# GpSimd's integer sums of the weight conversion in four pieces of 256 columns each

## The chip, the core and the metric

The kernel runs as one program on one core of a Trainium2 chip. The metric is the device time of an execution in microseconds (us). A core has five engines that work through their own instruction queues in order: TensorE (PE in the profile, with PEld for its weight loads), VectorE (DVE), ScalarE (ACT), GpSimd (POOL) and SyncE (SP), which issues most of the DMA transfers here.

## What is computed

Three parts follow each other: attention in which each row keeps its 32 largest scores, a dense layer with a gate, and a layer with eight experts of which each token uses two.

```python
scores = scale * np.matmul(q, k.transpose(0, 1, 3, 2))          # 4 batches, 8 heads, 576 tokens, 64
kth = np.partition(scores, -32, axis=-1)[..., -32:-31]
scores = np.where(scores >= kth, scores, -1e9)
attn = np.exp(scores - max); attn = attn / (sum + 1e-09)
x = attn @ v                                                     # 2304 x 512
h = x @ w_in                                                     # w_in 512 x 2048
x = (h * np.clip(h + 3.0, 0.0, 6.0) / 6.0) @ w_out               # w_out 2048 x 512
logits = x @ w_gate + log1p(exp(x @ w_noise)) * noise            # top 2 of 8 experts per token
out[token] += weight * (np.maximum(x[token] @ w1[e], 0) @ w2[e]) # for its two experts e
```

`w_in` and `w_out` reach the kernel as 64-bit floats. [...]

## The kernel before

The program has a phase A (attention and the dense layer, about the first 880 us) and a phase B (the experts). A scheduler puts the instructions of each engine into a fixed order before the program runs. It places them by its own times for each instruction, so that a change of a few instructions may move many others.

Phase A goes in steps of one slot, 144 in all: a slot is one head for 128 tokens. In a step PE makes the scores (L295), ACT copies them (L304, tile `ss`), and DVE finds the 32 largest: seven maxima over segments (L313, `seg`), a chain of maxima and replacements (L319 to L323, tile `a`), a mask of what lies below (L340, `z`), a maximum over that (L352), the choice of the threshold (L356) and the masking of the exponentials (L365, `e`). GpSimd helps each step with small work: the bias of the exponential (L328, `a`), the product of mask and scores (L346, `y`), sums and reciprocals (L370, L373, `sum` and `rb`), and the low halves of values that are split into two fp32r numbers (L213 for `k`, L268 for `q`, L426 and L438 for the output of attention).

The dense layer goes in blocks of 128 of its 2048 hidden columns, 16 blocks (`fb`). Between steps 4 and 19 the weights of one block per step are converted by `Weights.convert`: two DMAs bring a tile `wraw` of 128 x 1024 pairs of words; DVE makes the upper word's bits (L117 with its result in `wt`, L118, twice each, 512 columns at a time); ACT turns the lower word into an integer (L120); GpSimd adds the two as integers (L121). Then `Weights.split` makes a rounded copy on ACT (L130) and what is left with two matmuls and a copy (L138 to L140). Eleven of the blocks are stored to DRAM (`wscr`) and loaded again by SP for each use (`w_fetch`, L450, tile `ws`, four buffers); five stay in SBUF. From step 25 on, PE works on one block of one group of tokens per step (L464 into `h`, L505 into `xa`) beside the attention. The loads of `k` (L203, L204), `v` (L218, L220) and `q` (L261) go through the same SP queue; a batch's eight heads of `k` are loaded at the steps where its first tokens come up.

Phase B multiplies the gathered tokens of each expert with its weights (L880, L904).

Of the kernel before, what the change touches and what calls it, by code (L numbers as in the profile page):

```python
# [13 lines left out]
ALU = mybir.AluOpType  # L14
# [61 lines left out]
class Weights:  # L76
# [27 lines left out]
    def convert(self, fb):  # L104


        if not self.f64:
            return
        nc, t = self.nc, self.raws[fb]
        if self.small:  # L110
            m = self.ap.tile([128, 1024], F32, name=f"wm{fb}", tag="wm", bufs=1)
            nc.vector.tensor_scalar(m.bitcast(I32), t[:, :, 1], 0x7FFFFFFF, None, op0=ALU.bitwise_and)
            nc.vector.tensor_scalar(m, m, TINY, None, op0=ALU.is_ge)
        for i in range(2):
            hi = t[:, 512 * i:512 * i + 512, 1]
            tmp = self.ap.tile([128, 512], I32, name=f"wt{fb}_{i}", tag="lx", bufs=LXB)
            nc.vector.tensor_scalar(tmp, hi, 3, 0x3FFFFFF8, op0=ALU.logical_shift_left, op1=ALU.bitwise_and)  # L117
            nc.vector.scalar_tensor_tensor(hi, hi, -0x40000000, tmp, op0=ALU.bitwise_and, op1=ALU.bitwise_or)  # L118
        lo = t[:, :, 0]
        nc.scalar.activation(lo, lo.bitcast(U32), AF.Copy, scale=2.0 ** -29)  # L120
        nc.gpsimd.tensor_tensor(t[:, :, 1], t[:, :, 1], t[:, :, 0], op=ALU.add)  # L121
        if self.small:

            nc.vector.tensor_tensor(t.bitcast(F32)[:, :, 1], t.bitcast(F32)[:, :, 1], m, op=ALU.mult)
# [1144 lines left out]
```

## Time and profile before

| what | value |
|---|---|
| median of 3 runs | 1406.64 us (1406.3 to 1410.03) |
| the profiled execution's own time | 1411.69 us |
| its span in the profile | 1409.9 us |
| PE busy | 1302.8 us (92% of the span) |
| DVE busy | 1004.1 us (71%) |
| POOL busy | 818.2 us (58%), 1151 instructions |
| ACT busy | 745.0 us (53%) |
| chain that ended last, by engine | PE 56%, DVE 26%, DMA 5%, POOL 4%, ACT 4% |

The span is what the profile covers, from the first instruction to the last; the execution's own time is 1.8 us longer. Shares over the whole span hide the stages: PE is the busiest engine over all, yet in the first 200 us it is not. So the rows below are mostly of stretches. A busy time counts an instruction from its start to its end, also while it is held up in the engine.

### The profile page before, as it was taken

To read this page: it belongs to the slowest core of one execution; us is meant where nothing else is said; L and a number is where in the kernel's file an instruction comes from. 1 tells how busy PE (TensorE), PEld (TensorE's weight loads), DVE (VectorE), ACT (ScalarE), POOL (GpSimd) and SP (SyncE) were. 2 spreads that over 40 slices of the span, in tenths; PEclk is the share of its full clock that TensorE was granted. 3 is DMA by queue.
4 is the path that set the end of the run, shared out by engine and by line. 5 is a ranking of instruction groups with operands and counts; after the bars stand their busy time and mean duration, and the time that the engine had idled before them with its cause. 6 is when DMAs were issued, how large, how long until landed. Compare 5 with 4: busy or idle time off the path is not lost.

```text
span 1409.9 us, 26993 instructions
## 1 busy us (share of the span) xinstructions
PE 1302.8 (92%) x9006; PEld 1128.9 (80%) x9006; DVE 1004.1 (71%) x3827; ACT 745.0 (53%) x1565; POOL 818.2 (58%) x1151
## 2 busy tenths in 40 slices
PE   5767899999999979999899999899999999999996
PEld 3545688888888868898688888778889888898985
DVE  7999997899998899986999983456353534444241
ACT  6867766667676756666676654435222322223220
POOL 7666666676666778665587864233214556465461
PEclk9888999999999989999999999999999999999998
DMA  7766645445355614445233547756446555465431
GB/s 234 262 242 218 250 170 196 155 144 172 130 179 193 222 12 156 163 171 200 70 128 136 150 143 257 236 167 210 134 147 193 170 171 188 146 216 174 144 110 38
DMA packets 138101, 239.57 MB, mean 170 GB/s; under 512 B 39779, under 2 KB 93155, under 8 KB 123872
## 3 DMA queue, kind: packets, MB, share of 16 engines
q1 hardware_dynamic: 127600, 210.57, 45.3%
q0 software_dynamic: 10352, 27.18, 5.8%
q8 instruction: 73, 1.20, 0.4%
q14 instruction: 76, 0.62, 0.1%
HBM read 209.08 MB, written 31.64 MB: 171 GB/s over the span
## 4 chain that ended last, share of the span: by engine, by line
PE 56%; DVE 26%; DMA 5%; issue 4%; POOL 4%; ACT 4%; SPq 1%; POOLq 0%; DVEq 0%; ACTq 0%
PE ac L904 15%; PE hb L880 15%; PE h L464 7%; PE xa L505 7%; DVE seg L313 5%; DVE e L365 5%; DVE a L352 4%; DVE z L340 3%; PE s L295 3%; PE av L416 3%; PE pa L384 2%; DVE a L356 2%; DVE r L480 1%; POOL idw L758 1%; PE et L844 1%
## 5 line engine op out<-in xcount | busy, mean ns | idle before, releaser
L904 PE MATMUL ac<-w,hh 128*128 128x512 f32 x960 | 249.0, 401 | 4.9 <-issue 3.6
L880 PE MATMUL hb<-xe,w 128*128 128x320 f32 (+2 forms) x1536 | 239.8, 311 | 1.0 <-DVE hh L887 0.5
L880 PEld LDWEIGHTS hb<-xe,w 128*128 128x128 f32 x1536 | 232.5, 189 | 10.1 <-issue 3.9
L346 POOL TENSOR_TENSOR y<-z,ss 128x576 f32<-128x576 bf16 x144 | 192.5, 1337 | 56.5 <-DVE z L340 49.6
L904 PEld LDWEIGHTS ac<-w,hh 128*128 128x128 f32 x960 | 173.5, 189 | 44.3 <-ACT hh L886 5.0
L887 DVE SCALAR_TENSOR_TENSOR hh<-hb,hh 128x640 fp32r<-128x640 f32 (+2 forms) x72 | 53.9, 749 | 213.6 <-ACT hh L886 176.7
L886 ACT ACTIVATE hh<-hb 128x640 fp32r<-128x640 f32 (+2 forms) x72 | 46.6, 647 | 292.2 <-PE hb L880 264.6
L313 DVE MAX8 seg<-ss 128x8 f32<-128x82 f32 (+1 forms) x1008 | 166.7, 228 | 20.6 <-ACT ss L304 20.2
L464 PE MATMUL h<-xT,ws 128*128 128x256 f32 x1188 | 164.2, 286 | 7.5 <-DVE r L480 7.4
L505 PE MATMUL xa<-ws,g 128*128 128x512 f32 x594 | 166.6, 404 | 1.9 <-ACT g L187 1.8
L464 PEld LDWEIGHTS h<-xT,ws 128*128 128x128 f32 x1188 | 149.3, 189 | 15.3 <-DVE r L480 12.3
L866 POOL TENSOR_TENSOR w<-r,w 128x1024 fp32r<-128x1024 f32 x40 | 98.4, 2465 | 84.5 <-ACT w L864 77.1
L365 DVE SCALAR_TENSOR_TENSOR e<-ss,thrs,e 128x576 f32<-128x576 f32 x144 | 141.3, 982 | 0.5
L335 ACT ACTIVATE e<-ss,a 128x576 f32<-128x576 f32 x144 | 113.9, 791 | 32.1 <-POOL a L328 30.9
L304 ACT COPY ss<-s 128x576 f32<-128x576 f32 x144 | 92.5, 642 | 65.3 <-PE s L389 45.8
L352 DVE MAX8 a<-y 128x8 f32<-128x576 f32 x144 | 108.0, 750 | 23.1 <-POOL y L346 22.9
L493 POOL TENSOR_TENSOR g<-r,g 128x256 fp32r<-128x256 f32 x124 | 96.1, 775 | 36.5 <-ACT g L187 23.1
L340 DVE TENSOR_SCALAR_CACHE_REDUCE z<-ss,a 128x576 bf16<-128x576 f32 x144 | 115.4, 801 | 1.0
L505 PEld LDWEIGHTS xa<-ws,g 128*128 128x128 f32 x594 | 102.2, 189 | 17.2 <-ACT g L187 2.1
L384 PE MATMUL pa<-ident,e 128*128 128x128 f32 x576 | 92.9, 285 | 24.1 <-DVE e L365 21.0
L295 PE MATMUL s<-kt,qt 128*128 128x288 f32 x512 | 102.0, 323 | 10.6 <-ACT ph L397 5.7
L920 POOL DMA_INDIRECT out_dram<-y,id x40 | 41.9, 1048 | 115.6 <-DVE y L919 91.6
(217 smaller groups left out, 2645.5 us busy)
## 6 DMA issues: line engine op xcount, KB each, us to landing
ws<-wscr SPq DMA_DIRECT2D x99, 1024.0 KB
r<-in_moe_w_dram SPq DMA_DIRECT2D x144, 256.0 KB
wscr<-wsp SPq DMA_DIRECT2D x11, 1024.0 KB
wraw<-in_moe_w_in_dram SPq DMA_DIRECT2D x16, 512.0 KB
wraw<-in_moe_w_out_dram SPq DMA_DIRECT2D x16, 512.0 KB
ck<-in_moe_w_in_dram SPq DMA_DIRECT2D x32, 256.0 KB
ck<-in_moe_w_out_dram SPq DMA_DIRECT2D x32, 256.0 KB
out_dram<-zero SPq DMA_DIRECT2D x18, 256.0 KB
```

Of the source, the lines that this page charges most:

```text
L295: nc.tensor.matmul(p[:, half, 0:288], qt[:, j, :], KT[b, h][:, half * 288:(half + 1) * 288], start=(m == 0), stop=(m == n - 1))
L313: nc.vector.max(ST[i][:, j, :], SS[i][:, edge[j]:edge[j + 1]])
L335: nc.scalar.activation(e, SS[i], AF.Exp, bias=A8[i][:, 24:25], scale=0.125)
L340: TS(z, SS[i], A8[i][:, 7:8], None, op0=ALU.is_lt, op1=ALU.add, accum_out=A8[i][:, 26:27])
L346: nc.gpsimd.tensor_tensor(y, Z.pop(i), SS[i], op=ALU.mult)
L352: nc.vector.max(A8[i][:, 8:16], Y.pop(i))
L365: STT(E[i], SS.pop(i), thrs[:, i:i + 1], E[i], op0=ALU.is_ge, op1=ALU.mult, accum_out=SUM[i // 2][:, i % 2:i % 2 + 1])
L384: nc.tensor.transpose(p[:, j * 128:(j + 1) * 128], e[:, j * 128:(j + 1) * 128], ident)
L464: o = nc.tensor.matmul(p[:, 0:n], w[:, a, d, :], xt[b][:, d, 0:n], start=(m == 0), stop=(m == 11))
L505: nc.tensor.matmul(ACC[t], g[:, a, j * 128:(j + 1) * 128], w[:, b, :], start=(fb == 0 and m == 0), stop=(fb == NFB - 1 and m == 2))
L880: o = nc.tensor.matmul(p[:, half, 0:hn], w[:, a, d, :], XE[job][:, b, d, half * hn:(half + 1) * hn], start=(m == 0), stop=(m == 11))
L904: o = nc.tensor.matmul(ACC[job, j], h[:, a, j * 128:(j + 1) * 128], w[:, b, :], start=(x % NF2 == 0 and m == 0), stop=(x % NF2 == NF2 - 1 ...
```

## The change

The one integer addition of 1024 columns per block becomes four of 256 columns.

```diff
         lo = t[:, :, 0]
         nc.scalar.activation(lo, lo.bitcast(U32), AF.Copy, scale=2.0 ** -29)
-        nc.gpsimd.tensor_tensor(t[:, :, 1], t[:, :, 1], t[:, :, 0], op=ALU.add)
+
+        for i in range(0, 1024, 256):
+            nc.gpsimd.tensor_tensor(t[:, i:i + 256, 1], t[:, i:i + 256, 1], t[:, i:i + 256, 0], op=ALU.add)
```

The columns, the values and the waits ahead of the first addition are the same. In the changed kernel each line from the addition on has a number higher by two: L123 is the addition, L348 is what was L346, and so on. A number behind a tile's name counts what was built and has no other meaning.

The order of GpSimd's queue around the blocks 4 and 5. Before:

```order
L328 TENSOR_SCALAR a83_397<-a83_397 128x1
L121 TENSOR_TENSOR wraw4_529<-wraw4_529 128x1024
L373 TENSOR_SCALAR rb0_416<-sum0_341 128x128
L346 TENSOR_TENSOR y2_364<-z2_339,ss2_251 128x576
L346 TENSOR_TENSOR y3_451<-z3_411,ss3_308 128x576
L213 TENSOR_TENSOR ksb0_103<-kr6_236,ksb0_103 128x4x64
L213 TENSOR_TENSOR ksb0_103<-kr6_236,ksb0_103 64x64
L328 TENSOR_SCALAR a84_486<-a84_486 128x1
```

With the change:

```order
L330 TENSOR_SCALAR a83_400<-a83_400 128x1
L372 TENSOR_SCALAR sum0_341<-sum0_341 128x2
L123 TENSOR_TENSOR wraw4_538<-wraw4_538 128x256 x2
L348 TENSOR_TENSOR y2_367<-z2_339,ss2_251 128x576
L123 TENSOR_TENSOR wraw4_538<-wraw4_538 128x256 x2
L375 TENSOR_SCALAR rb0_419<-sum0_341 128x128
L348 TENSOR_TENSOR y3_457<-z3_414,ss3_308 128x576
L330 TENSOR_SCALAR a84_492<-a84_492 128x1
```

The four pieces stand as two and two, with a product `y` between them (with an L375 or an L330 in other blocks); 12 of the 16 blocks have such a break, the others stand as four in a row.

The scheduler also moves work far behind the conversion, up to the last steps of phase A; phase B has the order that it had. PE's queue around the scores of the last slot (s143). Before:

```order
L464 MATMUL h7_8_12782<-xT7_10859,ws7_8_12523 128x256 x10
L295 MATMUL s143_12720<-kt31_9830,qt143_12643 128x288 x4
L389 MATMUL s143_12720<-ident_66,e138_12442 128x128
L464 MATMUL h7_8_12782<-xT7_10859,ws7_8_12523 128x256 x2
L505 MATMUL xa14_12256<-ws7_7_12435,g7_7_12775 128x512 x3
L505 MATMUL xa15_12260<-ws7_7_12435,g7_7_12775 128x512 x3
L674 MATMUL lg13_12894<-wgn_948,lx13_12844 128x16 x2
L384 MATMUL pa139_12725<-ident_66,e138_12442 128x128 x4
L674 MATMUL lg13_12894<-wgn_948,lx13_12844 128x16 x2
L464 MATMUL h7_9_12855<-xT7_10859,w9_1199 128x256 x12
```

With the change:

```order
L507 MATMUL xa14_12304<-ws7_8_12571,g7_8_12897 128x512 x3
L297 MATMUL s143_12768<-kt31_9878,qt143_12691 128x288 x4
L507 MATMUL xa15_12308<-ws7_8_12571,g7_8_12897 128x512 x3
L466 MATMUL h7_10_12953<-xT7_10907,ws7_10_12742 128x256 x11
L386 MATMUL pa139_12773<-ident_66,e138_12490 128x128 x4
L391 MATMUL s143_12768<-ident_66,e138_12490 128x128
L466 MATMUL h7_10_12953<-xT7_10907,ws7_10_12742 128x256
L507 MATMUL xa14_12304<-w9_1229,g7_9_12950 128x512
L665 MATMUL lt13_12887<-ident_66,xm13_12215 128x128 x4
```

`h7_10` is the dense layer's block 10 of token group 7. Before, the last scores stand within block 8, and block 9 follows; with the change block 10 follows.

SP's queue where a `k` of the last batch is loaded (kr25). Before:

```order
L203 DMA kr24_8761<-in_k_dram 128x256
L204 DMA kr24_8761<-in_k_dram 64x64
L450 DMA ws3_15_7384<-wscr_78 128x2048
L450 DMA ws4_1_7559<-wscr_78 128x2048
L203 DMA kr25_8852<-in_k_dram 128x256
L204 DMA kr25_8852<-in_k_dram 64x64
L261 DMA qr11_1_7645<-in_q_dram 128x4x64
```

With the change:

```order
L452 DMA ws3_14_7336<-wscr_78 128x2048
L205 DMA kr24_8809<-in_k_dram 128x256
L206 DMA kr24_8809<-in_k_dram 64x64
L205 DMA kr25_8900<-in_k_dram 128x256
L206 DMA kr25_8900<-in_k_dram 64x64
L452 DMA ws3_15_7432<-wscr_78 128x2048
L263 DMA qr11_1_7693<-in_q_dram 128x4x64
L452 DMA ws4_1_7607<-wscr_78 128x2048
```

The load of kr25 stood behind two loads of the dense layer's weights (ws3_15, ws4_1); it stands ahead of both now.

## Rows read from the trace of the kernel before

**Rows 1.** Busy time of each engine by stretch: us, PE, PEld, DVE, ACT, POOL, clock, DMA share, GB/s

```profile
50.00:157.00 107.00, 76.38 (x435) 52.53 (x434) 104.27 (x380) 78.26 (x151) 68.42 (x86) 0.87 0.64 228
335.00:840.00 505.00, 477.25 (x3887) 421.75 (x3885) 457.98 (x2087) 337.11 (x799) 351.46 (x589) 0.98 0.44 146
840.00:945.00 105.00, 98.35 (x603) 84.86 (x600) 42.60 (x126) 45.92 (x86) 35.27 (x62) 0.97 0.68 214
```

**Rows 2.** Single lines of DVE, whole span: ns shortest/median/longest, first and last start

```profile
L117 DVE TENSOR_SCALAR wt<-wraw x32: 396/422/2214, 9.1 to 148.6; 128x512 int32<-128x512 int32 x32
L118 DVE SCALAR_TENSOR_TENSOR wraw<-wraw,wt x32: 666/678/2072, 9.5 to 152.1; 128x512 int32<-128x512 int32 x32
L356 DVE SCALAR_TENSOR_TENSOR a<-rank,a x144: 201/230/2650, 24.5 to 837.1; 128x9 f32<-128x9 f32 x144
L365 DVE SCALAR_TENSOR_TENSOR e<-ss,thrs,e x144: 790/815/2743, 25.1 to 837.3; 128x576 f32<-128x576 f32 x144
L313 DVE MAX8 seg<-ss x1008: 215/228/249, 12.3 to 827.4; 128x8 f32<-128x82 f32 x120, 128x8 f32<-128x83 f32 x48
```

**Rows 3.** Timeline of DVE, from 53 to 148 us: start us, us, instruction

```profile
53.65 2.65 DVE L356 SCALAR_TENSOR_TENSOR a<-rank,a 128x9 f32<-128x9 f32 x1
...
62.40 1.65 DVE L118 SCALAR_TENSOR_TENSOR wraw<-wraw,wt 128x512 int32<-128x512 int32 x1
...
100.35 1.85 DVE L356 SCALAR_TENSOR_TENSOR a<-rank,a 128x9 f32<-128x9 f32 x1
...
107.30 1.05 DVE L356 SCALAR_TENSOR_TENSOR a<-rank,a 128x9 f32<-128x9 f32 x1
...
124.96 1.67 DVE L117 TENSOR_SCALAR wt<-wraw 128x512 int32<-128x512 int32 x1
...
132.04 1.23 DVE L365 SCALAR_TENSOR_TENSOR e<-ss,thrs,e 128x576 f32<-128x576 f32 x1
...
145.24 2.34 DVE L365 SCALAR_TENSOR_TENSOR e<-ss,thrs,e 128x576 f32<-128x576 f32 x1
```

**Rows 4.** Timeline of POOL at three of these places

```profile
53.97 0.45 POOL L426 TENSOR_TENSOR xs<-xs 128x128 f32<-128x128 f32 x1
54.39 1.88 POOL L121 TENSOR_TENSOR wraw<-wraw 128x1024 int32<-128x1024 int32 x1
...
61.42 2.08 POOL L121 TENSOR_TENSOR wraw<-wraw 128x1024 int32<-128x1024 int32 x1 [2.60 <-ACT ksb L187]
63.46 1.73 POOL L346 TENSOR_TENSOR y<-z,ss 128x576 f32<-128x576 bf16 x1
...
146.93 0.97 POOL L426 TENSOR_TENSOR xs<-xs 128x128 f32<-128x128 f32 x1
```

**Rows 5.** Single lines of POOL, whole span, columns as in rows 2

```profile
L121 POOL TENSOR_TENSOR wraw<-wraw x16: 1884/1894/2403, 11.8 to 153.5; 128x1024 int32<-128x1024 int32 x16
...
L268 POOL TENSOR_TENSOR qsb<-qr,qsb x36: 721/739/1384, 4.4 to 772.1; 128x256 fp32r<-128x256 f32 x36
...
L426 POOL TENSOR_TENSOR xs<-xs x72: 452/463/983, 54.0 to 849.9; 128x128 f32<-128x128 f32 x72
```

**Rows 6.** Chain of waits that ended last: start us, us, what

```profile
20.61 2.20 POOL wraw L121
...
837.20 1.68 PE h L464 x12
...
852.66 1.41 PE h L464 x12
854.07 1.39 PE xa L505 x6
```

**Rows 7.** Waits by total, 160 to 850 us: us, times, longest

```profile
DVE a L352 <- POOL y L346: 22.9, 22, 3.4
```

**Rows 8.** Timeline of SP's queue: ws3_15 and ws4_1, then kr25

```profile
464.41 3.98 SPq L450 DMA_DIRECT2D ws<-wscr  x2
470.52 0.33 SPq L203 DMA_DIRECT2D kr<-in_k_dram  x1
```

## The prediction

> **What bounds the kernel now.** I read the busy times by stretch first, to see which engine is full where the additions run. All 16 start between 11.8 and 153.5 us [rows 5]. From 50 to 157 us DVE is busy for 104.27 of 107 us, POOL for 68.42 and PE for 76.38 [rows 1]. In that stretch DVE sets the pace; GpSimd has a third of its time free. From 335 to 840 us PE (477 of 505) and DVE (458) are both nearly full and take turns, and from 840 to 945 us PE is full (98 of 105) [rows 1]. The chain of waits says the same: near 837 us it passes from DVE to PE and stays there for the rest of the dense layer [rows 6].
>
> Next I looked at what DVE's full time consists of, in the durations of single lines. L313 has 215 ns at its shortest and 249 at its longest. L356, which writes nine columns, takes 201 ns at its shortest and 2650 at its longest; L117 goes from 396 to 2214, L118 from 666 to 2072, L365 from 790 to 2743 [rows 2]. So some lines of DVE are held up inside the instruction and others never. The timelines show by what: L356 starts at 53.65 us and lasts to 56.30, and on POOL the addition runs from 54.39 to 56.27 [rows 3, 4]. DVE comes free when GpSimd's instruction ends. The other way round as well: the addition from 61.42 to 63.50 holds L118, L118 then runs, and the product behind the addition takes 1.73 us; behind the addition at 145 us L426 takes 0.97 where its shortest is 0.452 [rows 4, 5]. The two engines take turns at something that both use, an instruction at a time.
>
> From 50 to 157 us, seven of DVE's instructions are held by an addition. Each one's time less the shortest of its line [rows 2, 3]: 62.40: 1.65 - 0.67 = 0.98; 100.35: 1.85 - 0.20 = 1.65; 107.30: 0.85; 124.96: 1.67 - 0.40 = 1.27; 132.04: 1.23 - 0.79 = 0.44; 145.24: 2.34 - 0.79 = 1.55. At 53.65 other GpSimd work holds L356 too, so I count the addition's own 1.88 [rows 4]. The sum is **8.6 us** of the pacing engine's time.
>
> **The change, part by part.**
>
> Price of a piece. The trace has no integer addition of 256 columns. Below it cannot cost less than a quarter of the whole, 1.884 / 4 = 0.47 us. Above I take the other two-input operation of 256 columns, L268 with 0.72 [rows 5]. L426 with 128 columns takes 0.452 [rows 5], so 128 columns more cost 0.269 and a fixed share of 0.452 - 0.269 = 0.18 us is left. The addition's 1.884 less 0.18 makes 1.70 for 1024 columns, 0.43 for 256: a piece is **0.61 us**. It is the nearer value, being the addition's own rate per column. Four pieces take 2.44, 0.55 more than one addition; 16 x 0.55 = 8.8 us of POOL time (between 0 and 16 x 1.0 = 16). It lies in a stretch where GpSimd is idle for 38.6 of 107 us [rows 1], and the copy L130 on ACT, which waits for the sum, stands a step later in the program. If that cover were gone, DVE's wait for `y` at L352 would show it, which is 22.9 us in all and in the later stretch [rows 7]. Once, at 20.61 us, an addition is itself a link of the chain [rows 6]: **+0.6 us** there.
>
> What the pieces take away. An instruction of DVE that comes while an addition runs waits to its end. With pieces it can come in between two of them, if it is let in. Two things bound this. If DVE comes in at each boundary, it waits for half a piece on average, 0.3 us; seven stalls make 2.1, and 6.5 us are saved. If it never comes in while GpSimd has work ready, the stall lasts until the last piece of a row of them: nothing is saved, and the 0.55 of the longer conversion is added to it, 7 x 0.55 = 3.9 us at most. The rows show both. At 62.40 and 145.24 DVE was let in at the end of the addition, ahead of work that was ready. At 53.65 it was not: L426 started at 53.97 and the addition at 54.39, both after L356 had started, and both at their normal length [rows 3, 4]. I take one piece, 0.6 us, for each of the seven: half a piece on average and every second time half a piece more than that, and in 12 of 16 blocks another instruction breaks the row of pieces as well. That is 7 x 0.6 = 4.2 left of 8.6, **4.4 us saved**.
>
> The Trainium skill, in "SBUF — State Buffer", section "Who interferes with whom", says that DVE and GpSimd share one pair of ports under an exclusive lock, that whoever issues first has it for the whole instruction, and that an instruction of DVE with two SBUF inputs is among those that need it. Read so that a waiting instruction is next at each end, this would give the 6.5 us. The stall at 53.65 agrees with the lock but not with a turn at each end, so the row decides and I stay at 4.4.
>
> What the scheduler moved. PE's queue: of the dense layer, 278 matmuls of L464 and 150 of L505 stood behind the last scores, 264 and 141 stand there now. Twelve of L464 take 1.41 us and six of L505 take 1.39 [rows 6]: 14 x 0.118 + 9 x 0.232 = 3.7 us of PE work that no longer lies behind the end of attention, where PE is the bound. It has to be done before that, beside DVE, where PE has 28 us free of 505 [rows 1]. All of it is gained if attention ends as early as now; nothing if PE's extra work holds attention up by as much. I take half, **1.9 us**. SP's queue: kr25 now stands ahead of ws3_15 and ws4_1. In the trace kr25 left at 470.52, the two weight loads between 464.41 and 468.39 [rows 8]. It waits for a buffer that GpSimd frees, so the two would leave some 6 us later than now. Four buffers of weights ahead hide that; I count nothing for it, and price it below.
>
> Sum: -4.4 + 0.6 - 1.9 = -5.7 us. The profiled execution took 1411.69 us and would take 1406.0. It lies 5.05 above the median of the runs, 1406.64, for which the same difference makes **1400.9 us**.
>
> About 0.3%, 4.2 us, is what can be told from no change here.
>
> **The rivals.**
>
> 1. DVE is let in at each boundary and all of the tail's 3.7 us is gained: 0.6 - 6.5 - 3.7 = -9.6, 1397.0 us. For it speak the turns at 62.40 and 145.24, against it the one at 53.65.
>
> 2. No change that can be told. DVE's 4.4 us are saved but PE, nearly full from 335 us on, does not start its stretches earlier, because the order there is another one with waits of its own. Then between -4.2 and +4.2 is left. For it: PE and DVE both over 90% busy from 335 to 840, so that an order that is a little worse takes back what a few us at the start gave.
>
> 3. Slower, by GpSimd keeping its turn. Four pieces ready in a row are then one addition of 2.44 us. A longer one meets more of DVE's instructions and holds each longer: both grow by 2.44 / 1.88 = 1.3, so the 8.6 us become 8.6 x 1.69 = 14.5, +5.9, with the +0.6 of the start: 1413.1 us. It decides if a stall behind pieces is over 1.2 us on average (8.6 / 7) and no less frequent. For it: 53.65; against it: the breaks in 12 of 16 blocks.
>
> 4. Slower, by SP's queue. Loads of weights stand behind loads of `k` and `v` that wait for a buffer. One delay of 6 us that PE sees in full makes 1406.6 - 5.7 + 6 = 1406.9, two make 1412.9. It decides from the point at which a weight load lands after PE asks for its block. For it: such exchanges stand at each of the three changes of batch. Against it: the four buffers, and that a `k` that comes earlier also ends a wait of attention.
>
> **How the numbers follow.** The forecast has 0.36 and the first rival 0.10; both are faster by over 0.3%, together 0.46. The second rival has 0.31. The third has 0.10 and the fourth 0.13, together 0.23 for slower. The range reaches from 1395, a little under the first rival's 1397.0, since the new order alone may be worth a few us, up to 1411: that leaves out most of the third rival and the two-delay case of the fourth, about 0.13, and 0.07 below. The forecast's own range is 1397 to 1402.4.
>
> **What would show it.** The piece's line should have 64 instructions of 0.55 to 0.72 us. In the stretch from 50 to some 155 us L356, L117, L118 and L365 should show the seven stalls at 0.3 to 0.9 us each where they had up to 1.9; L313 should not change. The last addition should then start some 4 us earlier than 153.5, and attention's last L365 earlier than 837.1. GpSimd should be busy for about 6 us more in that stretch and idle for over 25. The forecast is wrong if stalls of over 1.5 us behind runs of pieces are left (the third rival), if the first stretch ends earlier and the end of attention does not (the second), or if PE's L464 waits for `ws` loads (the fourth).

## The result, and the profile after

The changed kernel takes 1393.5 us in the median of 4 runs (1388.65 to 1396.62). Run beside it, the kernel before takes 1408.34 us (4 runs, 1406.3 to 1411.43). The ratio is 0.989, with a 95% interval of 0.9854 to 0.9926: 14.8 us, or 1.1%, faster. The forecast of 1400.9 us had the sign, and less than half of the size.

The profiled execution took 1393.8 us, its span is 1391.6. The page gives PE 1296.8 us (93%), DVE 994.3 (71%), POOL 834.5 (60%, 1199 instructions) and ACT 745.4. Of the chain that ended last PE now has 65% and DVE 21%, where they had 56 and 26.

Three points of phase A show where the time went. They are the end of L365 (L367 now) of slot 24, when all weights are converted; its end in slot 143, when attention is over; and the start of the last matmul of L464 (L466), the first product of the dense layer.

| us from the start | before | after | difference |
|---|---|---|---|
| slot 24, L365 ends | 186.1 | 176.3 | -9.8 |
| slot 143, L365 ends | 838.1 | 828.8 | -9.3 |
| last L464 starts | 903.8 | 888.4 | -15.4 |

So 9.8 us are won in the first 180 us. They are kept through the 650 us behind them, and 6.1 more are won between the end of attention and the end of the dense layer. What follows the last point, phase B for the most part, whose order did not change, differs by 2.9 us between these two executions; such a difference also stands between runs of one kernel.

These are the single lines, with the columns of [rows 2] and [rows 5]. The sum is L123, and L117, L118, L358 and L367 are the lines that were held up; L315 is the one that never was:

```profile
L123 POOL TENSOR_TENSOR wraw<-wraw x64: 602/612/1220, 11.2 to 143.1; 128x256 int32<-128x256 int32 x64
...
L117 DVE TENSOR_SCALAR wt<-wraw x32: 402/566/1805, 8.5 to 139.4; 128x512 int32<-128x512 int32 x32
L118 DVE SCALAR_TENSOR_TENSOR wraw<-wraw,wt x32: 665/714/1644, 8.9 to 141.6; 128x512 int32<-128x512 int32 x32
...
L358 DVE SCALAR_TENSOR_TENSOR a<-rank,a x144: 204/230/2031, 25.2 to 827.8; 128x9 f32<-128x9 f32 x144
L367 DVE SCALAR_TENSOR_TENSOR e<-ss,thrs,e x144: 792/812/2277, 28.4 to 828.0; 128x576 f32<-128x576 f32 x144
...
L315 DVE MAX8 seg<-ss x1008: 216/228/250, 11.7 to 818.9; 128x8 f32<-128x82 f32 x120, 128x8 f32<-128x83 f32 x48
```

A piece takes 0.612 us in the median. The last one starts at 143.1, where the last addition started at 153.5 [rows 5]; the last L367 starts at 828.0, where it was 837.1 [rows 2]. L315 has 216 to 250 ns, as before. The medians of L117 and L118 went up (566 and 714 from 422 and 678) while their longest went down: more instructions are held, each for a shorter time.

The busy times by stretch, in the columns of [rows 1]:

```profile
50.00:157.00 107.00, 80.00 (x463) 54.95 (x461) 106.28 (x414) 83.75 (x161) 83.48 (x125) 0.84 0.70 250
335.00:840.00 505.00, 482.49 (x3932) 429.37 (x3932) 448.17 (x2063) 337.28 (x801) 348.65 (x590) 0.98 0.46 152
840.00:945.00 105.00, 97.35 (x557) 83.72 (x556) 45.11 (x127) 43.94 (x78) 35.29 (x59) 0.95 0.66 205
```

In the first stretch DVE does 414 instructions in 106.3 us where it did 380 in 104.3: it is as full as it was, and gets through more. POOL goes from 68.4 to 83.5 us and still has 23 us free. From 335 us on PE does 482 us of work where it did 477 [rows 1]: work of the dense layer has come forward.

How the first 180 us became shorter can be read from the four lines that can be held, as groups from the start to the end of slot 24 (busy us, mean ns of one; then idle time of DVE ahead of them and what ended it). Before:

```profile
L365 DVE SCALAR_TENSOR_TENSOR e<-ss,thrs,e 128x576 f32<-128x576 f32 x25 | 28.4, 1135 | 0.0
L118 DVE SCALAR_TENSOR_TENSOR wraw<-wraw,wt 128x512 int32<-128x512 int32 x32 | 24.9, 779 | 0.1
L117 DVE TENSOR_SCALAR wt<-wraw 128x512 int32<-128x512 int32 x32 | 23.7, 741 | 8.9 <-DMA wraw<-in_moe_w_in_dram 8.6 <-DMA wraw<-in_moe_w_out_dram 0.3
...
L356 DVE SCALAR_TENSOR_TENSOR a<-rank,a 128x9 f32<-128x9 f32 x25 | 15.8, 632 | 0.0
```

After:

```profile
L118 DVE SCALAR_TENSOR_TENSOR wraw<-wraw,wt 128x512 int32<-128x512 int32 x32 | 26.7, 834 | 0.1
L367 DVE SCALAR_TENSOR_TENSOR e<-ss,thrs,e 128x576 f32<-128x576 f32 x25 | 25.5, 1018 | 0.0
L117 DVE TENSOR_SCALAR wt<-wraw 128x512 int32<-128x512 int32 x32 | 23.9, 747 | 6.5 <-DMA wraw<-in_moe_w_in_dram 6.2 <-DMA wraw<-in_moe_w_out_dram 0.3
...
L358 DVE SCALAR_TENSOR_TENSOR a<-rank,a 128x9 f32<-128x9 f32 x25 | 9.0, 358 | 0.0
```

The four groups together take 92.8 us before and 85.1 after, with as many instructions: 7.7 us less. DVE's idle time goes from 12.0 to 9.4 us; nearly all of that is the wait for `wraw` ahead of L117 (8.9 to 6.5). The rest of DVE's work is 81.3 and 81.8. That is the 9.8 us.

The timelines show a run of pieces. POOL from 59 us:

```profile
59.10 2.38 POOL L123 TENSOR_TENSOR wraw<-wraw 128x256 int32<-128x256 int32 x3
...
61.73 1.71 POOL L123 TENSOR_TENSOR wraw<-wraw 128x256 int32<-128x256 int32 x2
```

DVE over the same time:

```profile
59.21 1.06 DVE L118 SCALAR_TENSOR_TENSOR wraw<-wraw,wt 128x512 int32<-128x512 int32 x1
60.19 0.83 DVE L117 TENSOR_SCALAR wt<-wraw 128x512 int32<-128x512 int32 x1
...
61.73 0.67 DVE L118 SCALAR_TENSOR_TENSOR wraw<-wraw,wt 128x512 int32<-128x512 int32 x1
62.32 0.57 DVE L358 SCALAR_TENSOR_TENSOR a<-rank,a 128x9 f32<-128x9 f32 x1
```

L118 is held for 0.39 us (1.06 - 0.67) and L117 for 0.43, each inside a run of pieces, and each runs before the next piece: three pieces take 2.38 us instead of 1.84. A stall here is an instruction's time over the shortest of its line, where that is over 0.08 us, and it is put down to the GpSimd instructions that ran meanwhile. Counted over the whole start, DVE's stalls while a sum runs fall from 12.0 us in 11 stalls (longest 2.45) to 7.5 us in 26 (longest 0.43). In the prediction's own stretch, from 50 to 157 us, they fall from 8.5 to 5.0 us, in 17 stalls now; ahead of 50 us they fall from 3.5 to 2.6.

### The profile page after: what moved, and what is told of

Its sections match the earlier page's. It is cut to its first block, busy times and chain, and to the rows that moved or that the text cites. A ratio compares the mean times of both kernels' runs of the same rounds, so it can differ in the third digit from the quotient of the medians.

```text
span 1391.6 us, 27045 instructions
## 1 busy us (share of the span) xinstructions
PE 1296.8 (93%) x9006; PEld 1127.7 (81%) x9006; DVE 994.3 (71%) x3827; ACT 745.4 (54%) x1565; POOL 834.5 (60%) x1199
## 4 chain that ended last, share of the span: by engine, by line
PE 65%; DVE 21%; issue 4%; POOL 3%; DMA 3%; ACT 2%; SPq 0%; POOLq 0%; DVEq 0%; ACTq 0%
PE hb L882 15%; PE ac L906 15%; PE h L466 10%; PE xa L507 9%; PE av L418 4%; DVE seg L315 4%; PE s L297 4%; DVE e L367 3%; DVE z L342 3%; PE pa L386 3%; DVE a L354 2%; DVE wraw L118 1%; DVE wt L117 1%; DVE a L358 1%; PE et L846 1%
## 5 line engine op out<-in xcount | busy, mean ns | idle before, releaser
L348 POOL TENSOR_TENSOR y<-z,ss 128x576 f32<-128x576 bf16 x144 | 193.6, 1345 | 43.8 <-DVE z L342 40.0
L315 DVE MAX8 seg<-ss 128x8 f32<-128x82 f32 (+1 forms) x1008 | 165.7, 228 | 17.2 <-ACT ss L306 16.8
L466 PE MATMUL h<-xT,ws 128*128 128x256 f32 x1188 | 165.2, 287 | 7.8 <-DVE r L482 6.5
L507 PE MATMUL xa<-ws,g 128*128 128x512 f32 x594 | 163.5, 401 | 3.4 <-ACT g L189 2.4
L466 PEld LDWEIGHTS h<-xT,ws 128*128 128x128 f32 x1188 | 150.4, 190 | 15.0 <-DVE r L482 11.0
L367 DVE SCALAR_TENSOR_TENSOR e<-ss,thrs,e 128x576 f32<-128x576 f32 x144 | 135.3, 939 | 0.2
L354 DVE MAX8 a<-y 128x8 f32<-128x576 f32 x144 | 108.1, 751 | 24.0 <-POOL y L348 23.5
L337 ACT ACTIVATE e<-ss,a 128x576 f32<-128x576 f32 x144 | 113.4, 788 | 15.4 <-POOL a L330 14.4
```

Of the source, the lines that this page charges most:

```text
L315: nc.vector.max(ST[i][:, j, :], SS[i][:, edge[j]:edge[j + 1]])
L337: nc.scalar.activation(e, SS[i], AF.Exp, bias=A8[i][:, 24:25], scale=0.125)
L348: nc.gpsimd.tensor_tensor(y, Z.pop(i), SS[i], op=ALU.mult)
L354: nc.vector.max(A8[i][:, 8:16], Y.pop(i))
L367: STT(E[i], SS.pop(i), thrs[:, i:i + 1], E[i], op0=ALU.is_ge, op1=ALU.mult, accum_out=SUM[i // 2][:, i % 2:i % 2 + 1])
L466: o = nc.tensor.matmul(p[:, 0:n], w[:, a, d, :], xt[b][:, d, 0:n], start=(m == 0), stop=(m == 11))
```

## The experiments

Two theories. **The pieces**: VectorE is let in between them, and what it saves there is the gain; the order matters little. **The order**: the scheduler, given other instructions, made another order for all engines, and that order is the gain; the pieces matter little. A third possibility is that neither does it alone.

To tell them apart, the order of every engine was taken from the two kernels as a table (all but the sums) and laid on other versions by added ordering edges without waits. So the sums can be cut in any way while everything else keeps its place. The first four kernels ran on one chip; the other eight ran on another on which the kernel before takes 1420 us instead of 1407. So ratios are compared here, each against the kernel before on its own chip, and of the traces the points in phase A. The ratios given are not always the quotients of the two medians; on the second chip, where the kernel before scatters from 1415 to 1431 us, they lie up to 0.4% apart. The diffs leave out the lines by which the table finds the sums. Those lines move the numbers: L120, L121, L361 and L370 are what L117, L118, L356 and L365 were before, L125 is the sum, L351 the product `y`, L357 the maximum behind it, and L375 and L376 are the former L370 and L371.

### Four pieces in the old order

```diff
-        nc.gpsimd.tensor_tensor(t[:, :, 1], t[:, :, 1], t[:, :, 0], op=ALU.add)
+        for i in range(0, 1024, 256):
+            nc.gpsimd.tensor_tensor(t[:, i:i + 256, 1], t[:, i:i + 256, 1], t[:, i:i + 256, 0], op=ALU.add)
...
+        pin(tc)      # the order of the kernel before, the four pieces in the place of the sum
```

> The four pieces stand in a row where the one sum stood; every other instruction of every engine keeps the order of the kernel before. Theory A, the pieces themselves: VectorE's stalls behind the sums fall from 12 us to about 8 up to slot 24, as in the changed kernel, and what follows from it at the start is kept: 5 to 10 us faster than before, 1398 to 1403 us. Theory B, the new order of everything else: the pieces alone are worth their stalls at most, and the 0.55 us more per conversion takes some of that back: 0 to 4 us faster, 1404 to 1408 us.

Measured: 1403.88 us against 1406.75, ratio 0.9983 (0.9968 to 0.9997). Slot 24 ends at 180.3 (-5.8 against before), slot 143 at 830.8, the last L464 at 898.0 (-5.8). The pieces alone give some 60% of the gain at the start; of the tail they give nothing (67.1 us from the end of attention to the last L464, where it was 65.7). In the runs' median only 2.9 us are left of it. That time lies between the two expected ranges.

### One sum in the new order

```diff
-        for i in range(0, 1024, 256):
-            nc.gpsimd.tensor_tensor(t[:, i:i + 256, 1], t[:, i:i + 256, 1], t[:, i:i + 256, 0], op=ALU.add)
+        nc.gpsimd.tensor_tensor(t[:, :, 1], t[:, :, 1], t[:, :, 0], op=ALU.add)
...
+        pin(tc)      # the order of the changed kernel, one sum in the place of the first piece
```

> One sum of 1024 columns, where the first of the four pieces stands in the changed kernel; every other instruction of every engine keeps the order of the changed kernel. Theory A: the stalls of 1 to 2 us come back and with them the time at slot 24; the order is worth 4 us at most: 1403 to 1408 us. Theory B: most of the 14.8 us stays: 1394 to 1399 us.

Measured: 1405.21 us, ratio 0.9989 (0.9976 to 1.0002). Slot 24 ends at 186.6 (+0.6) and slot 143 at 838.0; the last L464 at 899.1 (-4.7). The order alone gives nothing at the start, and most of the tail: 61.1 us there. The waits of DVE in the first 190 us of this kernel, as totals (us, times, longest):

```profile
DVE wt L120 <- DMA wraw<-in_moe_w_in_dram: 5.3, 2, 5.1
DVE sum L376 <- POOL sum L375: 4.4, 2, 2.3
DVE seg L318 <- ACT ss L309: 1.9, 2, 1.3
DVE a L357 <- POOL y L351: 1.7, 2, 0.9
```

The second row is new; before and after the change there is no such wait in this stretch. POOL's timeline shows one of its two times:

```profile
100.83 2.35 POOL L125 TENSOR_TENSOR wraw<-wraw 128x1024 int32<-128x1024 int32 x1 [2.35 <-ACT e L340]
103.27 0.19 POOL L375 TENSOR_SCALAR sum<-sum 128x2 f32<-128x2 f32 x1
```

and DVE's its end:

```profile
103.49 0.17 DVE L376 RECIPROCAL sum<-sum 128x2 f32<-128x2 f32 x1 [2.05 <-POOL sum L375]
```

A 0.19 us instruction of GpSimd stands behind a whole sum, and DVE waits 2.05 us for it. In the changed kernel such small instructions stand between two pieces in many blocks, and these waits are not there.

### One sum at the last piece's place, four pieces in a row, and the two kernels again

The next two keep the new order as well. One has the whole sum where the last piece stood. The other has the four pieces in a row where the first stood. The last two lay the old and the new table on the kernels that they came from, so that any cost of the table itself would show.

```diff
+        pin(tc)      # the changed kernel's order; the sum at the last piece's place
+        pin(tc)      # the changed kernel's order; four pieces in a row at the first one's place
```

> The changed kernel's order with one sum of 1024 columns where the last of the four pieces stands, so that the small work that stands between the pieces goes ahead of the sum. Theory A: the stalls of VectorE behind sums are those of one sum, 12 us, and the time is that of the one sum at the first place, 1403 to 1407 us. Theory B: the waits of 6 us at L371 and L352 are gone and slot 24 comes at 180 to 182 us in place of 186.6; 1398 to 1402 us.

> The changed kernel's order, but the four pieces of a block all stand where its first one stood, in a row, so that the products and sums that stood between them come up to 1.2 us later. Theory A, the shortness of the pieces is what counts: VectorE gets in between any two, stalls behind sums stay at 0.3 us each, 1392 to 1397 us. Theory B, what counts is that GpSimd's other small work gets in between: VectorE waits for it about as with one sum (4.4 us at the reciprocals L371, 1.7 at L352), slot 24 some 4 to 6 us later and 1397 to 1403 us.

> The kernel before, its order written out instruction by instruction: the same program. It shows how far two profiles of one program differ from stage to stage. Expected: the same time as before within 0.2%, slot 24 at 186 us and the last matmul of the dense layer's first product at 904 us, each within 2 us; a larger difference there would mean that the stage times read from single profiles are not to be trusted to that much.

> The changed kernel, its order written out: the same program. Expected: 1391 to 1397 us, slot 24 at 176 us, the last matmul of the first product at 888 us, each within 2 us.

Measured, against 1420.5 us: the kernel before by its table 1418.46, ratio 0.9995 (0.997 to 1.0019); the changed kernel by its table 1403.98, 0.9902 (0.9869 to 0.9935). So the table costs nothing that shows, and the gain is the same on the second chip within the intervals. The late sum has 1414.17, 0.9958 (0.993 to 0.9985), and four in a row 1410.84, 0.9942 (0.9919 to 0.9964).

The two kernels again also show how well the points in phase A repeat. The kernel before has 185.4, 836.4 and 902.2 us where it had 186.1, 838.1 and 903.8, and the changed kernel 175.6, 828.6 and 888.2 where it had 176.3, 828.8 and 888.4. The differences are -9.8, -7.8 and -14.0 us there, so the first point can be trusted to under 1 us and the others to about 2. What the second chip takes longer lies behind the last point: 516.4 us for the kernel before, against 506.1. The 1391 to 1397 us that were expected of the changed kernel did not allow for that.

The start of six kernels, split as above (us to the end of slot 24):

| kernel | four lines | DVE idle | rest | end |
|---|---|---|---|---|
| before | 92.8 | 12.0 | 81.3 | 186.1 |
| four pieces, old order | 87.4 | 11.6 | 81.3 | 180.3 |
| one sum, new order | 88.6 | 16.0 | 82.0 | 186.6 |
| one sum late, new order | 94.0 | 9.1 | 81.8 | 184.9 |
| four in a row, new order | 84.8 | 15.0 | 82.1 | 181.9 |
| changed kernel | 85.1 | 9.4 | 81.8 | 176.3 |

This settles the start. In the new order a whole sum costs in one way or the other. Early, it delays the small work of GpSimd and DVE waits (idle 16.0); late, it meets DVE's own instructions and they stall (94.0). Four pieces in a row cure the stalls and not the waits (84.8 and 15.0). Only pieces with GpSimd's small work between them have both low. The waits of DVE with four in a row, up to the end of slot 24, are:

```profile
DVE wt L120 <- DMA wraw<-in_moe_w_in_dram: 6.7, 2, 5.7
DVE sum L376 <- POOL sum L375: 2.9, 2, 1.6
DVE seg L318 <- ACT ss L309: 1.9, 2, 1.3
...
DVE a L357 <- POOL y L351: 0.9, 1, 0.9
```

The rows for L375 and `y` are not in the changed kernel's list: they are 3.8 of the 5.6 us by which it idles less. The others are `ss` (0.6 in the changed kernel) and `wraw` (6.2). The two theories fall as alternatives: pieces alone give 5.8 us at the start and the order alone -0.6, and together they give 9.8.

### Two and eight pieces in the new order

```diff
-        for i in range(0, 1024, 256):
+        for i in range(0, 1024, 512):      # and 128 in the other kernel
...
+        pin(tc)      # the changed kernel's order
```

> Two sums of 512 columns in the changed kernel's order. Theory A: a stall behind a sum lasts up to 1 us, between the one sum and the four pieces: the time lies between theirs, nearer to the four. Theory B: the number of pieces makes no difference over 3 us at a given order.

> Eight sums of 128 columns in the changed kernel's order. A stall behind a sum lasts 0.4 us at most, but GpSimd has 8 x 0.39 = 3.1 us per conversion where the four pieces take 2.44, 11 us more in all. Theory A: within 3 us of the four pieces, as what is won at the stalls is lost to more of them. Theory B: the same, within 3 us. Slower by over 5 us would mean that GpSimd's work has become a bound at the start.

Measured: 1394.84 us, 0.992 (0.9902 to 0.9938), and 1394.57, 0.9921 (0.9904 to 0.9938). Both have nearly the gain of four pieces. With two the stalls behind sums are 9.5 us in 17 and slot 24 ends at 178.1; with eight they are 4.6 us in 24, but DVE idles 13.8 us and slot 24 ends at 179.5. GpSimd is busy 151.0 us up to there, against 139.2 with four: the shorter stalls are paid for with a longer conversion. The shortest times of the line are 1028 ns for 512 columns and 388 for 128:

```profile
L125 POOL TENSOR_TENSOR wraw<-wraw x32: 1028/1039/1644, 11.5 to 144.5; 128x512 int32<-128x512 int32 x32
```

```profile
L125 POOL TENSOR_TENSOR wraw<-wraw x128: 388/398/1276, 12.5 to 146.8; 128x128 int32<-128x128 int32 x128
```

### Two and eight pieces in the scheduler's own order

```diff
-        for i in range(0, 1024, 256):
+        for i in range(0, 1024, 512):      # and 128 in the other kernel; no table
```

> Sums of 512 columns, twice per block, with the scheduler's own order. With the changed kernel's order two pieces took 0.992 of before. If a shorter hold and room for other work between are what counts: 0.990 to 0.995 of before. If the gain at the end of attention (6 us of dense-layer matmuls done earlier) is chance: that part may be missing, 0.994 to 0.999.

> Sums of 128 columns, eight per block, with the scheduler's own order. Stalls behind sums fall to some 5 us up to slot 24, GpSimd has 11 us more to do than with four pieces. 0.988 to 0.995 of before if the pieces count; the dense layer's tail again by chance.

Measured, against 1420.1 us: 1422.06 with two, ratio 0.9996 (0.9966 to 1.0026), and 1414.39 with eight, 0.9958 (0.9927 to 0.9989). Both lie above the ranges expected. The same cuts that gave 0.992 in the changed kernel's order give nothing, or half, in the order that the scheduler makes for them. Two pieces end slot 24 at 182.3 and slot 143 at 837.9; eight end them at 176.5 and 835.7. On this chip the kernel before has 185.4 and 836.4. So with eight most of the gain at the start is there (-8.9 us), and 8 us of it are lost again by the end of attention, which the changed kernel's order does not do. The tail has 63.0 and 63.8 us. With two the stalls behind sums are as many us as before (12.4 in 21, longest 1.88).

### The product `y` in two pieces

After the sums, the product L346 (L348) is GpSimd's longest instruction in attention, and DVE's stalls while it runs are 26.0 us over phase A of the changed kernel. The same cut there, in the changed kernel's order and in the scheduler's own:

```diff
-        nc.gpsimd.tensor_tensor(y, Z.pop(i), SS[i], op=ALU.mult)
+        z = Z.pop(i)
+        for c in range(0, 576, 288):
+            nc.gpsimd.tensor_tensor(y[:, c:c + 288], z[:, c:c + 288], SS[i][:, c:c + 288], op=ALU.mult)
```

> The changed kernel's order with the product of mask and scores (576 columns, once per slot, behind which VectorE stalls for 26 us up to the end of attention) in two pieces of 288 that stand in a row. If the shorter hold is worth what it was at the sums: those 26 us fall to some 14, and where VectorE sets the pace, about half of attention, 5 us come off: 0.4% faster than the changed kernel. The rival: GpSimd has 144 x 0.18 = 26 us more work and VectorE's waits for the product at L352 (23 us) grow by as much as the stalls fall: no difference, or up to 0.4% slower.

> The same two changes (sums in four pieces, product in two), with the order that the scheduler makes of it. If the pieces are what counts: as the run before, within 0.3%. If the order is: it may fall anywhere between 0.99 and 1.01 of the changed kernel.

Measured, against 1420.1 us: 1402.84 us, 0.9856 (0.9808 to 0.9904), and 1400.9, 0.9827 (0.9785 to 0.9869). The quotients of these medians are 0.9879 and 0.9865, and the changed kernel's, 1403.98 by 1420.5, is 0.9884. Both beat the kernel before. The first can't be told from the changed kernel. The second has the lowest time on this chip, 3 us under the changed kernel, but its interval touches the changed kernel's (0.9869 to 0.9935), so that lead is not shown. By its table, phase A runs as in the changed kernel on the same chip to within 0.5 us (175.6 and 175.1, 828.6 and 828.8, 888.2 and 888.5). The stalls while `y` runs fall from 25.8 to 18.4 us over phase A, not to the 14 expected, and DVE waits for `y` for 32.6 us from 160 to 850 us where the changed kernel has 23.5: the rival held. In the scheduler's own order, slot 143 ends at 821.3 and the last L464 starts at 884.8, 3.4 us ahead of the changed kernel.

## Why the prediction was too small

**What held.** DVE sets the pace in the first 160 us, and the sums hold it up. The piece was put at 0.61 us and takes 0.612. GpSimd's extra time is hidden: DVE waits for `y` for 23.5 us where it was 22.9 [rows 7], and GpSimd has 23 us left free in the first stretch. That extra is larger than the 8.8 us of the forecast: the 64 pieces take 46.8 us in all where the 16 sums took 31.9, since VectorE holds many of the pieces up (752 ns in the mean against 612 in the median). GpSimd's busy time in the first stretch grew by 15 us instead of 6; 10.0 of them are the sums, the rest is other work. The +0.6 us at 20.61 did not come: no addition stands in the chain of the changed kernel's first 60 us.

**The first step that failed: the term of -4.4 as all that the start can give.** It counted seven stalls behind sums and left everything else of DVE's start as it was. The start gave 9.8 us, against 4.4 less 0.6. Besides the 4.5 behind sums, 3.5 us of other stalls went (behind `y` from 13.5 to 11.9, behind other GpSimd work from 7.3 to 5.4), and 2.6 us of waits, nearly all for `wraw`. By the table the pieces take 5.4 us off the four lines in the old order too, but only 0.4 off the waits; the rest needs the new order, which one sum spoils. The moved instructions of the start were in the order that I read, and I gave that move no price of its own.

That the stalls behind sums fall by 4.5 us for a term of 4.4 is luck. The term was for 50 to 157 us, where they fall by 3.5 (8.5 to 5.0); the other 1.0 comes from stalls ahead of 50 us that I did not count. Its rule was wrong too. I took a stall of one piece for each of the seven: half a piece, and half a piece more every second time. The trace shows that VectorE gets in at the first boundary behind each piece (longest stall 0.43 us), as in the first rival, but that it is held 17 times in that stretch instead of seven.

The Trainium skill, in "SBUF — State Buffer", section "Who interferes with whom", has GpSimd's and VectorE's shared ports locked for one whole instruction, and only for VectorE's instructions with two inputs or in a two-port mode. The trace agrees: the stalls end at a piece's end, and L315, with one input, has 216 to 250 ns. L117, with one input too, is held, so by that rule it would have to run in a two-port mode. It takes 396 ns for the 512 columns for which L118 takes 666; no run here shows the mode itself.

**The second step that failed: the term of -1.9 for the tail.** It counted 14 L464 and 9 L505 from the order, 3.7 us, and took half. From the end of slot 143 to the last L464 the two kernels have (groups of PE, busy us, mean ns), before:

```profile
L464 PE MATMUL h<-xT,ws 128*128 128x256 f32 x174 | 23.3, 282 | 1.3 <-DVE r L480 1.3
L505 PE MATMUL xa<-ws,g 128*128 128x512 f32 x84 | 22.2, 398 | 0.0
L505 PE MATMUL xa<-w,g 128*128 128x512 f32 x36 | 9.9, 401 | 0.0
L464 PE MATMUL h<-xT,w 128*128 128x256 f32 x72 | 9.5, 281 | 0.0
```

and after:

```profile
L466 PE MATMUL h<-xT,ws 128*128 128x256 f32 x167 | 22.5, 283 | 1.2 <-DMA ws<-wscr 1.2
L507 PE MATMUL xa<-ws,g 128*128 128x512 f32 x72 | 18.8, 396 | 0.0
L507 PE MATMUL xa<-w,g 128*128 128x512 f32 x36 | 9.8, 401 | 0.0
L466 PE MATMUL h<-xT,w 128*128 128x256 f32 x60 | 8.0, 281 | 0.0
```

That is 246 and 120 before, 227 and 108 after: 19 and 12 matmuls less, 4.8 us without the overlap of their ends, and 1.2 us of smaller work, nearly all L416 (40 matmuls before, 24 after). The tail shrinks from 65.7 to 59.6 us. I counted from the last scores, but attention ends with the mask behind them, and PE goes on meanwhile. And the half was wrong: PE's extra work ahead of the end did not hold attention up, since from slot 24 to slot 143 both kernels take the same (652.0 and 652.5 us). The tail goes with the order alone: one sum in the new order has 61.1 us there, the late sum and four in a row 59.7.

**The rivals.** The first had the right mechanism for both terms, let in at each boundary and all of the tail; its 9.6 us were still 5.2 short of the 14.8, for the stalls and waits that no term held. The second fell: what was won by slot 24 was there at slot 143. With eight pieces in the scheduler's own order it was lost, so such a thing does happen. The third, GpSimd keeping its turn, did not come about behind pieces here, but it exists: see the last section. Of the fourth there is 1.2 us in the tail, L466 once waiting for `ws`, where before a wait of 1.3 us stood.

**What stays open.** The parts in phase A add up to 15.4 us and the runs to 14.8, so little is left for phase B. But for four pieces in the old order the runs show 2.9 us where phase A shows 5.8, and for one sum in the new order 1.5 where it shows 4.7. In phase B, PE, ACT and GpSimd have the same order in all of these kernels, and yet from the start of the last L464 to the end one trace of each has 506.1 us before, 497.9 with four pieces in the old order and 502.1 with one sum in the new. So single traces can't tell where those 3 us go, and it was not found. Nor was it shown why the scheduler's own orders for two and eight pieces lose between slot 24 and the end, only that they do, or why the wait for `wraw` is shorter in the new order.

## What to carry to other kernels

When two engines lock each other out for whole instructions, cutting the long ones of the engine with time to spare can help, and here more than half of what it gained came from what could then stand between the pieces: in the new order and on one chip, four pieces in a row ended the start 3.5 us earlier than the kernel before and four with small work between them 9.8. Where a scheduler makes the order, an edit of one line is two changes, and the second must be priced stage by stage: the end of each stage in both traces, and how much work of the next stage's full engine stands behind it. Fixing the order and changing only the instructions tells the two apart. Here the pieces alone took 2.9 us off the median, the order alone 1.5, and both together 14.8; in phase A alone it was 5.8, 4.7 and 15.4.

## What the runs showed of the hardware

GpSimd's integer addition costs the same per column at the four lengths measured: 388, 602, 1028 and 1884 ns at the shortest for 128, 256, 512 and 1024 columns. That is 1.67 ns a column and 0.175 us for each instruction.

VectorE is not always next at a boundary. In four pieces in the old order, POOL from 60 us:

```profile
60.19 2.31 POOL L125 TENSOR_TENSOR wraw<-wraw 128x256 int32<-128x256 int32 x4
62.47 1.29 POOL L351 TENSOR_TENSOR y<-z,ss 128x576 f32<-128x576 bf16 x1
63.70 0.33 POOL L1344 MEMSET none<- 128x288 f32 x1
```

and DVE:

```profile
60.99 3.31 DVE L121 SCALAR_TENSOR_TENSOR wraw<-wraw,wt 128x512 int32<-128x512 int32 x1
```

L121 waits 2.64 us (3.31 - 0.67) through the rest of the pieces and the product; the pieces run at full speed. It gets in as the MEMSET begins, which has no input. With eight pieces in the scheduler's own order an L117 started at 33.94 us and lasted 3.07, through GpSimd's work on `k`, a product and three pieces.

Most such cases start just ahead of a boundary. In the traces of twelve kernels of this study, I counted VectorE's held instructions that started while a two-input instruction of GpSimd ran with the next one directly behind it. Of some 100 that started less than 0.1 us before the boundary, about 90 were still held 0.25 us behind it; of some 700 that started earlier, about 50. The exact counts shift with where the boundary between two instructions is put. At 53.65 [rows 3] the next instruction of GpSimd was a small one-input one, so that stall is not in the count. The third rival's mechanism is real, but rare: and cutting an instruction into pieces does not by itself put VectorE next.
